# Block 3's transpose moved from TensorE to the DMA, and the first loads in another order

## The chip, the cores and the metric

One core of one Trainium2 chip. The metric is the device time of one execution in microseconds (us). Engines: PE is TensorE, DVE VectorE, ACT ScalarE, POOL GpSimd, SP SyncE; SP and ACT issue DMAs through hardware queues, POOL through a software queue.

## The reference, cut to what matters

```python
def reference(A_x, A_wqkv, A_wo, B_x, B_w_in, B_w_sp, B_b_sp, B_w_out):   # S = 2048, D = 512, bf16
    x = A_x
    xn = layernorm(x)
    q, k, v = split(xn @ A_wqkv)           # 32 heads of 16
    # each position attends to itself and 7 earlier ones, 2 apart
    logits = einsum(q, k[pos - 2 * w]) * 16 ** -0.5      # w = 0..7, masked below 0
    a = (softmax(logits) * v[pos - 2 * w]).sum(w) @ A_wo
    z = gelu(xn @ B_w_in)                  # 1792 columns
    z1, z2 = z[:, :896], layernorm(z[:, 896:])
    g = B_w_sp @ z2 + B_b_sp[:, None]      # 2048 x 2048
    return x + a + (z1 * g) @ B_w_out
```

## The kernel before, in words

The 2048 positions are 16 blocks of 128 rows; four blocks make a wave of 512 columns for the products that want positions in the free dimension. Every step is a task of a planner (`Plan`): an engine, a function that emits instructions, an estimated time, a priority (the smaller goes first), and what it reads and writes. `schedule` is a list scheduler run when the kernel is built. It fixes the order of the tasks on each engine and the PSUM banks they use; the chip then follows that order, each engine waiting for semaphores. A table `land` gives the planner landing times for the first loads, and chains of task names near the end of `build_kernel` fix the order at the start by hand.

The start, around the change:

- PE first runs eight dummy matmuls (`warm0` to `warm7`, six of 512 columns and two of 128; line 566).
- ACT's queue loads blocks 0 and 1 of x (`ldx0`, `ldx1`); SP's loads V's weights in two halves (`ldwv0`, `ldwv1`), block 2, z2's weights in two halves (`ldwin2a`, `ldwin2b`), blocks 3 to 7, Q's and K's weights (`ldq`, `ldk`, 512 KB each) and blocks 8 to 15.
- Each block is normalised on DVE: `bnst`, `bnag`, `vpe` (statistics), a power on POOL (`rstd`, line 618), `norm` (line 630). PE needs the normalised block turned, with the features in the partitions (`xnT`). For blocks 0 to NXT-1 = 3 PE turns it by four matmuls with the identity (`xTr`, line 585), and ACT copies it out of PSUM (`xTe`, line 593). For blocks from 4 on, SP issues a DMA transpose (`xTd`, line 624).
- For blocks 0 to 2, V is made ahead of the normalisation: PE turns the raw block (`xTx`, line 585 too), ACT copies it (`xTc`, line 612), PE multiplies by V's weights (`V0_0` and so on, line 673; a `cs` task at line 645 sums the weights' columns, and ACT copies that out as `cse`), and a DVE step (`fix`, line 682) puts the mean right.
- `z2_b_0`, `z2_b_1` (line 785) multiply block b by the two halves of z2's weights; ACT applies the gelu (`z2g`). `Q0_c`, `K0_c` (line 696) are Q and K of the first wave, four groups c; they need `xnT` of blocks 0 to 3 and Q's and K's weights. `Q1_c` and `K1_c` need blocks 4 to 7.

After that: products of Q and K on DVE and their sums over a head on PE (`red`, line 732), softmax, V gathered by DMA and multiplied on DVE (line 955), z1 (line 831), the big product with w_sp (line 927) and the output (lines 983 and 992). PE goes through them in the planner's order.

`bbc` and `w_sp` are loaded after the transposes in `lnd[NXT:]`, that is of blocks 4 to 15.

Of the kernel before, what the change touches and what calls it, by code (L numbers as in the profile page):

```python
# [36 lines left out]
class Plan:  # L37
# [85 lines left out]
    def schedule(self, dma_bw=300.0, xbar_bw=190.0, dma_lat=1300.0, dma_pre=400.0, issue=None, tol=40.0, land=None,  # L123
# [49 lines left out]
        while left:  # L173
            pick = None
            for e in ENGS:
                sc = []
                for t in cand[e]:
                    r = max(t.ready, free[e])
                    for b in t.banks:
                        if b.base is None:  # L180
                            p = place(b)
                            if p is None:
                                r = None
                                break
                            r = max(r, p[2])
                    if r is not None:
                        sc.append((r, t))
                if not sc:
                    continue
                st = min(r for r, _ in sc)  # L190
                near = [(t.prio, t.idx, r, t) for r, t in sc if r <= st + tol]
                near.sort(key=lambda x: x[:2])
                r, t = near[0][2], near[0][3]
                if e == "act" and t.tbl is not None and tbl is not None and t.tbl != tbl:
                    stay = [x for x in near if x[3].tbl in (None, tbl)]
                    if stay and stay[0][0] < t.prio + t.late:
                        r, t = stay[0][2], stay[0][3]
                if pick is None or r < pick[0]:
                    pick = (r, e, t)
            if pick is None:  # L200
                raise RuntimeError("scheduler stuck")
            r, e, t = pick
            for b in t.banks:
                if b.base is None:
                    _, o, av = place(b)
                    b.base = o[0]
                    prevs = {id(slots[i]["prev"]): slots[i]["prev"] for i in o if slots[i]["prev"] is not None}
                    for pb in prevs.values():
                        for u in pb.users:
                            if u.eng == e == "pe":  # L210
                                t.odeps.add(u)
                            elif u is not t:
                                t.deps.add(u)
                    for i in o:
                        slots[i]["prev"] = b
            t.start = r
            if t.dma is not None:
                iss = issue[e]
                t.eng_end = r + iss
                bw = xbar_bw if t.dma.get("xbar") else dma_bw  # L220
                xs = max(r + iss + dma_pre, dma_free)
                xe = xs + t.dma["nbytes"] / (bw if xs > 7000.0 else min(bw, 265.0))
                dma_free = xe
                t.end = xe + dma_lat
                if t.name in land:
                    t.end = land[t.name]
                    dma_free = land[t.name] - 500.0
            else:
                dur = t.est
                if t.tbl is not None:  # L230
                    if tbl is not None and t.tbl != tbl:
                        dur += 1300.0
                    tbl = t.tbl
                t.end = r + dur
                t.eng_end = t.end - (overlap if e == "dve" else 0.0)
            free[e] = t.eng_end
            for b in t.banks:
                b.left -= 1
                if b.left == 0:
                    av = max(u.end + (220.0 if u.eng == "pe" else 60.0) for u in b.users)  # L240
                    for s in slots:
                        if s["prev"] is b:
                            s["avail"] = av
            cand[e].remove(t)
            order[e].append(t)
            left -= 1
            for o in t.outs:
                o.ready = max(o.ready, t.eng_end if t in o.odeps else t.end + hop(t, o))
                o.nwait -= 1
                if o.nwait == 0:  # L250
                    cand[o.eng].append(o)
# [87 lines left out]
def build_kernel(nc, A_x, A_wqkv, A_wo, B_x, B_w_in, B_w_sp, B_b_sp, B_w_out, out, report=False, emit=True):  # L339
# [8 lines left out]
    KP = 16  # L348
    NVS = 4
    NPB = 3  # L350
    NXT = 4
    NRAW = 3
    NWARM = 8
    x2 = A_x[0]
    o2 = out[0]

# [3 lines left out]
    off = {}  # L360
# [39 lines left out]
    with ExitStack() as es:  # L400
# [54 lines left out]
        R1(("yout", 3, 384), "yout", 128, 512 * 3 + 384)  # L455
        for s_ in range(NVS):
            R1(("Vs", s_), "Vs", 4096, 4096 * s_)
        R1(("wqk", 0), "wqk", 2048)
        R1(("wqk", 1), "wqk", 2048, 2048)
        for s_ in range(2):  # L460
            R1(("wv", s_), "wv", 1024, 1024 * s_)
        for r_ in range(NWS):
# [33 lines left out]

        def dma(eng, fn, nbytes, chan, reads=(), writes=(), name="", xbar=False, prio=0.0, after=()):
            return T(eng, fn, reads=reads, writes=writes, name=name, prio=prio, after=after,
                     dma=dict(chan=chan, nbytes=nbytes, xbar=xbar))

        ident = A("ident", 128)
        E32 = A("E32", 32)
# [35 lines left out]
                B_w_in[:, 1344:1792].rearrange("(c p) n -> p c n", p=128)),  # L538
                512 * 448 * 2, "w_in2b", writes=["w_in2b"], name="ldwin2b")

        def ld_wqk(which, eng):
            dma(eng, lambda e: e.dma_start(
                AC(off["wqk"] + 2048 * which, [[512, 4], [1, 512]]),
                A_wqkv[:, 512 * which: 512 * which + 512].rearrange("(c p) n -> p c n", p=128)),
                512 * 512 * 2, ("wqk", which), writes=[("wqk", which)], name="ld%s" % ("qk"[which]))

        dma("act", lambda e: e.dma_start(A("xin", 512), x2[0:128, :]), 128 * 512 * 2, ("xin", 0),
            writes=[("xin0", 0), ("xin0", 1)], name="ldx0")
# [1 line left out]
        ld_wv(0)  # L550
        ld_wv(1)
        ld_x(2, "sp")
        ld_win2a()
        ld_win2b()
        ld_x(3, "sp")
        ld_x(4, "sp")
        ld_x(5, "sp")
        ld_x(6, "sp")
        ld_x(7, "sp")
        ld_wqk(0, "sp")  # L560
        ld_wqk(1, "sp")

        bw = plan.bank("warm")
        for wi in range(NWARM):
# [14 lines left out]
        def pe_tr(src, keys, name):  # L579
            bk = plan.bank(name)  # L580

            def tr(t):
                last = None
                for dc in range(4):
                    last = t.matmul(P(bk, 128, 128 * dc), src[:, 128 * dc:128 * dc + 128], ident, start=True,  # L585
                                    stop=True)
                return last
            T("pe", tr, reads=keys + ["ident"], writes=[bk], est=(430.0 if name == "xTx0" else 4 * c_mm(128)), name=name)
            return bk

        def to_xnT(b, bk, halves, prio=0, after=()):
# [98 lines left out]
        def qk_pair(j, c):  # L690
            bk = plan.bank("QK%d_%d" % (j, c), 2)
            for which in range(2):
                def mm(t, which=which):
                    last = None
                    for dc in range(4):
                        last = t.matmul(P(bk, 512, 512 * which),  # L696
                                        AC(off["wqk"] + 2048 * which + 512 * dc + c, [[4, 128]]),
                                        AC(off["xnT"] + dc * S + 512 * j, [[1, 512]]), start=(dc == 0),
                                        stop=(dc == 3))
                    return last  # L700
                T("pe", mm, reads=[("wqk", which)] + [("xnT", b) for b in range(4 * j, 4 * j + 4)], writes=[bk],
                  est=4 * c_mm(512), name="%s%d_%d" % ("QK"[which], j, c), prio=10 + 18 * j + c)
            qo = off["QT"] + 2048 * (j % 2) + 512 * c
            ko = off["KT"] + c * (S + KP) + KP + 512 * j
# [183 lines left out]
        for j in range(NJ):  # L888
            for pr in PAIRS:
# [1 line left out]

        dma("sp", lambda e: e.dma_start(A("bbc", S), bass.AP(tensor=B_b_sp.tensor, offset=B_b_sp.offset,
                                                             ap=[[0, 128], [1, S]])),
            128 * S * 2, "bbc", writes=["bbc"], name="ldbbc", prio=7, after=lnd[NXT:])

        def ld_wT(tc):
            r_ = tc % NWS
            for p_ in range(4):
# [1 line left out]
                dma("sp", (lambda t0, p_: lambda e: e.dma_start_transpose(  # L900
                    AC(off["wT%d" % r_] + 128 * p_, [[512, NB], [1, 128]]), B_w_sp[t0: t0 + 128, :]))(t0, p_),
                    128 * S * 2, ("wT", p_), writes=[("wTs", r_, p_)], name="wT%d_%d" % (tc, p_), xbar=True,
                    prio=6 + tc, after=lnd[NXT:])

        dma("sp", lambda e: e.dma_start(A("w_out", FC * 512).rearrange("p (c n) -> p c n", c=FC),
                                        B_w_out.rearrange("(c p) n -> p c n", p=128)),
# [114 lines left out]

        byname = {t.name: t for t in plan.tasks}
        for names in (["warm%d" % wi for wi in range(NWARM)] +
                      ["xTx0", "cs_0", "V0_0", "xTx1", "cs_1", "V0_1", "xTx2", "V1_0", "V1_1", "xTr0", "V2_0", "V2_1", "xTr1",
                       "z2_0_0", "z2_0_0b", "z2_0_1", "xTr2", "z2_1_0", "z2_1_1", "xTr3", "z2_2_0"],
                      ("rstd4", "Vw0"),
                      ("bnst0", "bnag0", "vpe0", "bnst1", "bnag1", "vpe1", "norm0", "bnst2", "norm1", "bnag2", "vpe2", "norm2",
                       "bnst3", "bnag3", "vpe3", "bnst4", "norm3", "bnag4", "vpe4", "mr", "bnst5", "fix0", "fix1", "fix2"),
                      ["bnst%d" % b for b in range(5, NB)],
                      ("xTc0_0", "xTc0_1", "xTc1_0", "xTc1_1", "xTc2_0", "xTe0_0", "xTe0_2", "Ve0", "xTe1_0", "Ve1", "Ve2",  # L1030
                       "xTe2_0", "z2g0", "xTe3_0", "cse", "z2g1", "z2s0"), ("V10_1", "Q3_3")):
            for n0, n1 in zip(names, names[1:]):
                if byname[n0] not in byname[n1].deps:
                    byname[n1].odeps.add(byname[n0])

        plan.schedule(tol=20.0, dma_bw=300.0, dma_lat=1600.0, overlap=20.0,
                      land=dict(ldx0=3690.0, ldx1=4590.0, ldwv0=4220.0, ldwv1=5320.0, ldx2=5680.0, ldwin2a=8090.0,
                                ldwin2b=9300.0, ldx3=9750.0, ldx4=10060.0, ldx5=10440.0, ldx6=10820.0, ldx7=11250.0, ldq=12740.0, ldk=14220.0))
        if report:
            print("arena", AR, "fp", FR)  # L1040
            plan.report()
# [47 lines left out]
```

## Time and profile before

| | |
|---|---|
| time, median of 3 runs | 237.29 us (236.66 to 237.98) |
| the profiled execution | 236.69 us, span 235.1 us |
| PE busy | 232.2 us (99%) |
| DVE busy | 209.3 us (89%) |
| ACT busy | 97.0 us (41%) |
| DMA | 43.86 MB, mean 187 GB/s |

The profile is of one execution; times in it count from the start of its span, and the execution took 1.6 us more than the span. The busy share of PE counts from a matmul's start to its modelled end, so it says that PE always has a matmul in hand, not that it runs at its peak. A wait is named with what released it; idle time of an engine that holds up nobody costs nothing. A DMA that is issued runs later, so what counts for it is its landing.

### The profile page before, as it was taken

Reading aid. Unit: us, or ns where it says so; the run is one execution under the profiler, and the core shown is the slowest. Engines: PE = TensorE matmul, PEld = TensorE weight load, DVE = VectorE, ACT = ScalarE, POOL = GpSimd, SP = SyncE. Lnnn points to the kernel's source line nnn. Section 1 sums busy time; section 2 is a strip of 40 time slices with the busy share of each in tenths; the row PEclk is TensorE's granted clock in tenths of the full one; section 3 lists DMA queues with packets and bytes.
Section 4 is the critical chain, followed back from the end, with each engine's and each line's share of the span. In section 5 each row is a group of like instructions: output and inputs, shape, how many; then the busy total and the mean of one; then the engine's idle time right before and its main releaser. Section 6 shows DMA issues by size and latency. Waiting matters only on the chain.

```text
span 235.1 us, 3006 instructions
## 1 busy us (share of the span) xinstructions
PE 232.2 (99%) x1139; PEld 109.4 (47%) x1139; DVE 209.3 (89%) x271; ACT 97.0 (41%) x146; POOL 36.0 (15%) x56
## 2 busy tenths in 40 slices
PE   8999999999999999999999999999999999999996
PEld 3555555554444444444444444444444444444443
DVE  4698989999999999979999979989999798999632
ACT  4889889898868985410120134011111111000000
POOL 2268544230644300000000000000000000000000
PEclk9999999999999999999999999999999999999999
DMA  6997929998157314150869999999994949825532
GB/s 208 359 261 180 226 67 159 210 193 201 45 177 248 116 42 70 45 178 0 290 200 298 237 262 206 209 302 273 298 274 129 267 135 284 254 90 140 157 107 67
DMA packets 82013, 43.86 MB, mean 187 GB/s; under 512 B 54336, under 2 KB 81360, under 8 KB 82000
## 3 DMA queue, kind: packets, MB, share of 16 engines
q1 hardware_dynamic: 80768, 41.27, 69.9%
q0 software_dynamic: 800, 2.11, 2.8%
q10 hardware_dynamic: 432, 0.30, 0.4%
q8 instruction: 9, 0.15, 0.3%
q14 instruction: 4, 0.03, 0.0%
HBM read 26.35 MB, written 4.21 MB: 130 GB/s over the span
## 4 chain that ended last, share of the span: by engine, by line
PE 97%; DMA 1%; DVE 0%; issue 0%
PE ps L927 41%; PE ps L696 12%; PE ps L785 10%; PE ps L992 10%; PE ps L831 10%; PE ps L673 6%; PE ps L983 6%; DMA arena<-in_A_wqkv_dram 1%; PE ps L732 1%; PE ps L585 1%; PE ps L645 0%; DVE arena L998 0%
## 5 line engine op out<-in xcount | busy, mean ns | idle before, releaser
L927 PE MATMUL ps<-arena 128*128 128x512 bf16 x448 | 97.0, 379 | 0.0
L927 PEld LDWEIGHTS ps<-arena 128*128 128x128 bf16 x448 | 43.7, 98 | 53.1 <-issue 0.4
L935 ACT ACTIVATE arena<-ps 128x1024 bf16<-128x1024 f32 (+1 forms) x16 | 14.7, 916 | 77.0 <-PE ps L927 71.1
L955 DVE TENSOR_TENSOR arena<-arena 128x4096 bf16<-128x4096 bf16 x16 | 36.5, 2282 | 0.0
L717 DVE TENSOR_TENSOR arena<-arena 128x4096 bf16<-128x4096 bf16 x16 | 36.4, 2281 | 0.1
L958 DVE TENSOR_TENSOR arena<-arena 128x2048 bf16<-128x2048 bf16 (+1 forms) x32 | 30.2, 948 | 0.0
L696 PE MATMUL ps<-arena 128*128 128x512 bf16 x128 | 28.9, 379 | 0.0
L722 DVE TENSOR_TENSOR arena<-arena 128x4096 bf16<-128x4096 bf16 x12 | 27.5, 2288 | 0.1
L992 PE MATMUL ps<-arena 128*128 128x512 bf16 (+2 forms) x119 | 27.0, 366 | 0.0
L785 PE MATMUL ps<-arena 128*128 128x448 bf16 x128 | 25.8, 352 | 0.0
L831 PE MATMUL ps<-arena 128*128 128x512 bf16 x112 | 24.5, 379 | 0.0
L696 PEld LDWEIGHTS ps<-arena 128*128 128x128 bf16 x128 | 14.5, 113 | 13.1
L998 DVE TENSOR_TENSOR arena<-ps,arena 128x512 bf16<-128x512 f32 (+2 forms) x17 | 11.2, 657 | 9.0 <-PE ps L992 8.6
L705 ACT ACTIVATE arena<-ps 128x1024 bf16<-128x1024 f32 x16 | 16.3, 1021 | 3.6 <-PE ps L696 3.3
L785 PEld LDWEIGHTS ps<-arena 128*128 128x128 bf16 x128 | 12.4, 98 | 11.5
L992 PEld LDWEIGHTS ps<-arena 128*128 128x128 bf16 x119 | 11.4, 98 | 12.9
L831 PEld LDWEIGHTS ps<-arena 128*128 128x128 bf16 x112 | 11.0, 98 | 13.2 <-ACT arena L837 0.3
L983 PE MATMUL ps<-arena 128*128 128x512 bf16 (+2 forms) x68 | 16.6, 366 | 0.0
L793 ACT ACTIVATE arena<-ps 128x896 bf16<-128x896 f32 x16 | 14.6, 916 | 3.8 <-PE ps L785 3.7
L673 PE MATMUL ps<-arena 128*128 128x512 bf16 x64 | 16.1, 379 | 0.0
L938 DVE TENSOR_TENSOR arena<-arena 128x1024 bf16<-128x1024 bf16 (+1 forms) x16 | 9.9, 621 | 6.8 <-ACT arena L935 6.8
L837 ACT ACTIVATE arena<-ps 128x1024 bf16<-128x1024 f32 (+1 forms) x16 | 13.9, 922 | 4.9 <-PE ps L831 4.8
(62 smaller groups left out, 180.5 us busy)
## 6 DMA issues: line engine op xcount, KB each, us to landing
arena<-vscr SPq DMA_DIRECT2D x16, 1024.0 KB, 6.0
arena<-in_A_x_dram SPq DMA_DIRECT2D x30, 128.0 KB, 4.0
vscr<-arena POOLq DMA_DIRECT2D x16, 128.0 KB, 3.2
out_dram<-arena SPq DMA_DIRECT2D x15, 128.0 KB, 1.8
arena<-in_A_wqkv_dram SPq DMA_DIRECT2D x2, 512.0 KB, 6.4
arena<-in_B_w_in_dram SPq DMA_DIRECT2D x2, 448.0 KB, 5.6
arena<-in_B_w_in_dram SPq DMA_DIRECT2D x1, 896.0 KB, 6.1
arena<-in_B_w_out_dram SPq DMA_DIRECT2D x1, 896.0 KB, 4.9
```

Of the source, the lines that this page charges most:

```text
L673: last = t.matmul(P(bk, 512), A("xcT", 128, 512 * b + 128 * dc) if b < NRAW else xTv(b, dc), A("wv", 512, 512 * dc), start=(dc == 0), stop ...
L696: last = t.matmul(P(bk, 512, 512 * which), AC(off["wqk"] + 2048 * which + 512 * dc + c, [[4, 128]]), AC(off["xnT"] + dc * S + 512 * j, [[1 ...
L705: T("act", lambda a: a.activation(AC(qo, [[ko - qo, 2], [1, 512]]), P(bk, 1024).rearrange("p (t n) -> p t n", t=2), ACTF.Copy, scale=0.5), ...
L717: T("dve", (lambda pbv, qb, kb: lambda v: v.tensor_tensor(pbv, qb, kb, ALU.mult))(pbv, qb, kb), reads=rd, writes=[("pb", s_)], est=c_tt(40 ...
L722: T("dve", (lambda av, bv: lambda v: v.tensor_tensor(av, av, bv, ALU.add))(av, bv), reads=[("pb", 1)], writes=[("pb", acc)], est=c_tt(4096 ...
L785: last = t.matmul(P(bk, 448, 512 * hf), xTv(b, dc), AC(off["w_in2"] + 896 * dc + 448 * hf, [[1, 448]]), start=(dc == 0), stop=(dc == 3))
L831: last = t.matmul(P(bk, 512, 512 * i), AC(off["w_in1"] + 896 * dc + 128 * fc, [[1, 128]]), AC(off["xnT"] + dc * S + 512 * j, [[1, 512]]), ...
L927: last = t.matmul(P(bk, 512, 512 * i), AC(off["z2"] + FH * sh + 128 * fc, [[1, 128]]), AC(off["wT%d" % r_] + sh * 512, [[1, 512]]), start= ...
L955: T("dve", lambda v: v.tensor_tensor(tv, tv, av, ALU.mult), reads=[("attn", b)], writes=[("Vs", sv)], est=c_tt(4096), name="pv%d" % b, pri ...
L958: T("dve", (lambda n: lambda v: v.tensor_tensor(A("Vs", n, 4096 * sv), A("Vs", n, 4096 * sv), A("Vs", n, 4096 * sv + n), ALU.add))(n), wri ...
L983: last = t.matmul(P(bk, cn), AC(off["OT"] + 512 * tb + 128 * cc, [[1, 128]]), AC(off["wo"] + 512 * cc + c0, [[1, cn]]), start=(cc == 0), s ...
L992: last = t.matmul(P(bk, cn), AC(off["z1T"] + fc * S + 128 * tb, [[1, 128]]), AC(off["w_out"] + 512 * fc + c0, [[1, cn]]), start=False, sto ...
```

## The change

- Block 3 is turned by DMA instead of PE (`NXT` from 4 to 3). `lnd[4:]` keeps the order of the later loads behind the transposes of blocks 4 to 15.
- `ldx3` goes ahead of `ldwin2a` and `ldwin2b` on SP.
- Q's and K's weights come in one transfer of 1 MB, `ldqk`, laid out with Q and K side by side for each 128 rows, from ACT's queue, in ACT's order between `xTc2_0` and `xTe0_0`.
- On SP, `xTd3` goes after `ldx5` and ahead of `ldx6` and of all later blocks.
- Seven dummies instead of eight; the one that goes has 128 columns.
- The hand-written orders of PE, DVE and ACT are adapted.
- The planner asks for as many free pairs of banks as a task needs (before, one pair at a time), and its figures for DMA are others: transposes take SP 1270 or 2200 ns to issue and land 900 ns after their data, 270 instead of 300 GB/s for loads, another `land` table, a tolerance of 35 instead of 20 ns.

```diff
@@ Plan.schedule
-                    for b in t.banks:
+                    need = [b for b in t.banks if b.base is None]
+                    if len(need) > 1:
+                        ok = sorted(max(slots[i]["avail"], slots[i + 1]["avail"]) for i in (0, 2, 4, 6)
+                                    if all(slots[k]["prev"] is None or slots[k]["prev"].left == 0 for k in (i, i + 1)))
+                        r = max(r, ok[len(need) - 1]) if len(ok) >= len(need) else None
+                        need = []
+                    for b in need:
...
-                t.eng_end = r + iss
+                t.eng_end = r + (t.dma.get("iss") or iss)
...
-                t.end = xe + dma_lat
+                t.end = xe + (900.0 if t.dma.get("xbar") else dma_lat)
@@ build_kernel
-    NXT = 4
+    NXT = 3
-    NWARM = 8
+    NWARM = 7
...
-        R1(("wqk", 0), "wqk", 2048)
-        R1(("wqk", 1), "wqk", 2048, 2048)
+        R1("wqk", "wqk", 4096)
...
-                     dma=dict(chan=chan, nbytes=nbytes, xbar=xbar))
+                     dma=dict(chan=chan, nbytes=nbytes, xbar=xbar, iss=(1270.0 if nbytes < 400000 else 2200.0) if xbar else None))
...
-        def ld_wqk(which, eng):
-            dma(eng, lambda e: e.dma_start(
-                AC(off["wqk"] + 2048 * which, [[512, 4], [1, 512]]),
-                A_wqkv[:, 512 * which: 512 * which + 512].rearrange("(c p) n -> p c n", p=128)),
-                512 * 512 * 2, ("wqk", which), writes=[("wqk", which)], name="ld%s" % ("qk"[which]))
+        def ld_wqk(eng):
+            dma(eng, lambda e: e.dma_start(A("wqk", 4096).rearrange("p (c n) -> p c n", c=4),
+                                           A_wqkv[:, 0:1024].rearrange("(c p) n -> p c n", p=128)),
+                512 * 1024 * 2, "wqk", writes=["wqk"], name="ldqk")
...
         ld_x(2, "sp")
+        ld_x(3, "sp")
         ld_win2a()
         ld_win2b()
-        ld_x(3, "sp")
         ld_x(4, "sp")
         ld_x(5, "sp")
         ld_x(6, "sp")
         ld_x(7, "sp")
-        ld_wqk(0, "sp")
-        ld_wqk(1, "sp")
+        ld_wqk("act")
...
-            T("pe", tr, reads=keys + ["ident"], writes=[bk], est=(430.0 if name == "xTx0" else 4 * c_mm(128)), name=name)
+            T("pe", tr, reads=keys + ["ident"], writes=[bk], est=4 * c_mm(128), name=name)
...
-                                        AC(off["wqk"] + 2048 * which + 512 * dc + c, [[4, 128]]),
+                                        AC(off["wqk"] + 1024 * dc + 512 * which + c, [[4, 128]]),
...
-                T("pe", mm, reads=[("wqk", which)] + [("xnT", b) for b in range(4 * j, 4 * j + 4)], writes=[bk],
+                T("pe", mm, reads=["wqk"] + [("xnT", b) for b in range(4 * j, 4 * j + 4)], writes=[bk],
...
-            128 * S * 2, "bbc", writes=["bbc"], name="ldbbc", prio=7, after=lnd[NXT:])
+            128 * S * 2, "bbc", writes=["bbc"], name="ldbbc", prio=7, after=lnd[4:])
...
         for names in (["warm%d" % wi for wi in range(NWARM)] +
-                      ["xTx0", "cs_0", "V0_0", "xTx1", "cs_1", "V0_1", "xTx2", "V1_0", "V1_1", "xTr0", "V2_0", "V2_1", "xTr1",
-                       "z2_0_0", "z2_0_0b", "z2_0_1", "xTr2", "z2_1_0", "z2_1_1", "xTr3", "z2_2_0"],
+                      ["xTx0", "cs_0", "V0_0", "xTx1", "cs_1", "V0_1", "xTx2", "V1_0", "V1_1", "xTr0", "V2_0", "xTr1", "V2_1",
+                       "z2_0_0", "z2_0_0b", "z2_0_1", "xTr2", "z2_1_0", "z2_1_1", "z2_2_0", "z2_2_1"],
                       ("rstd4", "Vw0"),
-                      ("bnst0", "bnag0", "vpe0", "bnst1", "bnag1", "vpe1", "norm0", "bnst2", "norm1", "bnag2", "vpe2", "norm2",
-                       "bnst3", "bnag3", "vpe3", "bnst4", "norm3", "bnag4", "vpe4", "mr", "bnst5", "fix0", "fix1", "fix2"),
+                      ("bnst0", "bnag0", "vpe0", "bnst1", "bnag1", "vpe1", "norm0", "bnst2", "norm1", "bnag2", "vpe2", "bnst3", "norm2",
+                       "bnag3", "vpe3", "norm3", "bnst4", "bnag4", "vpe4", "mr", "bnst5", "fix0", "fix1", "fix2"),
                       ["bnst%d" % b for b in range(5, NB)],
-                      ("xTc0_0", "xTc0_1", "xTc1_0", "xTc1_1", "xTc2_0", "xTe0_0", "xTe0_2", "Ve0", "xTe1_0", "Ve1", "Ve2",
-                       "xTe2_0", "z2g0", "xTe3_0", "cse", "z2g1", "z2s0"), ("V10_1", "Q3_3")):
+                      ("xTc0_0", "xTc0_1", "xTc1_0", "xTc1_1", "xTc2_0", "ldqk", "xTe0_0", "xTe0_2", "xTe1_0", "Ve1", "Ve0", "Ve2",
+                       "xTe2_0", "z2g0", "cse", "z2g1", "z2s0"), ("ldx5", "xTd3", "ldx6"),
+                      *[("xTd3", "ldx%d" % b) for b in range(7, NB)], ("V10_1", "Q3_3")):
...
-        plan.schedule(tol=20.0, dma_bw=300.0, dma_lat=1600.0, overlap=20.0,
-                      land=dict(ldx0=3690.0, ldx1=4590.0, ldwv0=4220.0, ldwv1=5320.0, ldx2=5680.0, ldwin2a=8090.0,
-                                ldwin2b=9300.0, ldx3=9750.0, ldx4=10060.0, ldx5=10440.0, ldx6=10820.0, ldx7=11250.0, ldq=12740.0, ldk=14220.0))
+        plan.schedule(tol=35.0, dma_bw=270.0, dma_lat=1600.0, overlap=20.0,
+                      land=dict(ldx0=3600.0, ldwv0=4120.0, ldx1=4550.0, ldwv1=5230.0, ldx2=5600.0, ldwin2a=8250.0, ldx3=5950.0,
+                                ldwin2b=9450.0, csr=52000.0, ldx4=9850.0, ldx5=10400.0, xTd3=12700.0, ldqk=13300.0))
```

More of the change, by code (lines that the diff above doesn't have):

```diff
@@ L902, in ld_wT @@
                     128 * S * 2, ("wT", p_), writes=[("wTs", r_, p_)], name="wT%d_%d" % (tc, p_), xbar=True,
-                    prio=6 + tc, after=lnd[NXT:])
+                    prio=6 + tc, after=lnd[4:])
         dma("sp", lambda e: e.dma_start(A("w_out", FC * 512).rearrange("p (c n) -> p c n", c=FC),
```

## The prediction

> **What bounds the kernel now.** I read the page's busy shares and its chain first, to see which engine sets the end.
>
> ```profile
> PE 232.2 (99%) x1139; PEld 109.4 (47%) x1139; DVE 209.3 (89%) x271; ACT 97.0 (41%) x146; POOL 36.0 (15%) x56
> ...
> PE 97%; DMA 1%; DVE 0%; issue 0%
> ```
>
> TensorE (PE) is 97% of the chain; the other engines only matter where they make it wait. So the question is where PE waits. The chain of waits in order of time answers that for the start, which the change touches:
>
> ```profile
> 0.80 3.22 DMA arena<-in_A_wqkv_dram
> 4.02 0.05 issue
> 4.07 0.60 PE ps L645 x2
> ...
> 8.62 1.51 PE ps L785 x8
> ...
> 11.87 0.22 PE ps L585 x4
> 12.09 1.51 PE ps L785 x8
> 13.61 0.86 PE ps L673 x4
> 14.47 6.91 PE ps L696 x32
> ...
> 233.19 0.02 issue
> ```
>
> Until 4.02 the chain is V's first weight half landing; from 4.07 to 233.19 every piece is PE. The starts of single matmuls in the trace confirm it: after 4.07 none starts over 0.1 us later than the one before it allows. So a gain must be PE work removed or an earlier landing of V's weights, and any new wait on PE is lost whole. Next I read PE's timeline (start, us, what, idle before and its releaser) for the deadlines:
>
> ```profile
> 0.84 2.89 PE L566 MATMUL ps<-const-bfloat16-1.0 128*128 128x512 bf16 x8 [0.84 <-PEq L1074]
> 3.56 0.39 PE L585 MATMUL ps<-arena 128*128 128x128 bf16 x4
> ...
> 13.44 1.03 PE L673 MATMUL ps<-arena 128*128 128x512 bf16 x4
> ```
>
> Then ACT's and DVE's timelines at the places that the change moves, the landings of line 624 (the DMA transposes), and two stages of a table by microsecond (PEclk, DMA share, GB/s):
>
> ```profile
> 7.57 0.66 ACT L593 ACTIVATE arena<-ps 128x256 bf16<-128x256 f32 x2 [0.49 <-PE ps L585]
> ```
>
> ```profile
> 9.17 0.69 DVE L605 BATCH_NORM_STATS2 fpool<-arena 128x6 f32<-128x512 bf16 x1 [0.93 <-DMA arena<-in_A_x_dram]
> ```
>
> ```profile
> DMA to landing us min/median/max: 2.3/4.0/7.5
> ```
>
> ```profile
> 8.00:9.00 1.00, 1.00 1.07 373
> ...
> 11.00:12.00 1.00, 1.00 1.09 345
> ```
>
> ScalarE (ACT) and VectorE (DVE) have holes of 0.49 and 0.93 us; a DMA transpose takes 2.3 to 7.5 us from issue to landing; and the DMA engines are full. The landing times below are the trace's records of the semaphore increments.
>
> **The change part by part.**
>
> *xTr3 leaves PE.* Four 128-column matmuls, 0.22 us (piece "11.87"), leave a chain without slack: -0.22. Their eviction (0.60 us of ACT) goes too, which costs or gains nothing, since no PE piece waits for it.
>
> *One dummy fewer.* It is a 128-column one, 0.107 us apart from the next. The first real matmul starts at 3.56, x0 landed at 3.50, and the piece behind waits for V's weights until 4.02. Between -0.06 (starting on x0) and 0; since 4.02 stays, I take 0. The cover is the 0.28 us in which PE waits for those weights. The clock: dummies start every 427 ns, the first transposing matmuls every 56 ns, so full speed is there at 3.56 and the missing dummy is the last one at half speed. The Trainium skill ("TensorE: Matmul & The Clock Gate", Part 1) says that a free-running window of about 3.4 us of activity releases the clock; by that rule a shorter run-up may miss a window, which is the third rival. The trace has one such release and no missed one.
>
> *x3 ahead of z2's weights.* 131 KB at 373 GB/s puts both halves of z2's weights back by 0.35. The first landed at 7.52 and its first matmul starts at 8.46: covered by 0.94. The second landed at 8.77, hence 9.12; it is needed at 9.03 (weight load) to 9.21 (matmul of z2_0_1). Q and K's 1 MB on the other queue can overlap its tail: up to 0.3 more. The stall is 0 to 0.35; I take 0.10, nearer the lower end, because a transfer issued at 7.1 hardly has data moving before 8.9 (x1, issued at 1.26, needed 2.7 us to its first increment).
>
> *Q and K in one transfer on ACT's queue.* The issue (0.42 to 0.46 us as for x0 and x1) comes behind xTc2_0, which ends at 7.08, into the hole of 0.49 before xTe0_0 at 7.57: 0. If it took 0.9 (the longest issue among x's loads), xTe0_0 would be 0.4 late; z2_0_0 at 8.46 has 0.5 to spare. SP loses two issues. Landing: x0 to x5, V's and z2's weights had all landed at 9.90; 1.05 MB at 345 to 373 GB/s makes that 12.7 to 12.9, and xTd3 adds some 0.6 at most; with x6 and x7 ahead, K landed at 13.66 before. Needed by Q0 at 14.31 - 0.22 = 14.09: 0 cost, 0.4 to 1.4 to spare.
>
> *Block 3 by DMA.* DVE: bnst3 begins when x3 is there (5.84: x2 landed at 5.46, and the loads of x land 0.38 apart) and bnst2 is done, so bnst3 runs at about 7.15, norm2 ends at 8.25 as now (it waits for POOL's power), then bnag3, vpe3 (0.33), POOL 0.56 and norm3 0.41: done at 9.6, inside the hole of 0.93. SP issues xTd3 behind ldx5, whose issue was over at 5.55, so it waits for norm3, with x6 to x15 queued behind it. From 9.6 the row's 2.3 gives 11.9, its median 13.6; the first transpose of before (issued at 12.73, landed at 18.56, mixed with loads) gives 15.4. It needs 512 packets of 256 B at 18 ns, 0.6 us over 16 engines; alternating with the rest of Q and K's 1 MB it ends with that, about 13.2. V3 wants it at 13.44 - 0.22 = 13.22. Stall 0 to 2.2; I take 0.05, by the byte count.
>
> *x6 to x15 behind xTd3.* Ten loads at 0.44 (median) go out at 10.9 to 15.3, ahead of xTd4 to xTd7 by their priority (0 against 1); these go out at 15.3 to 20.4 instead of 12.7 to 19.2. QK of the second wave starts at 24.24 - 0.22 = 24.02 and needs block 7: about 21.5. Cost 0; the cover is z2_3 and z2_4 (3.0 us). By the longest row (7.5) it would land at 26.6, a stall of 2.6. Statistics of blocks 6 to 15 are up to 3 us later; DVE takes other work then, and its last sums wait for PE (9.0 us idle at line 998), so nothing on PE: 0.
>
> *The planner's figures and the bank rule.* Another order of the same PE work; it costs nothing unless a bank or an input is late. PE has no such wait now; below 0 is excluded, since there is none to remove. 0, at most the 1 us size of one late eviction.
>
> Sum: -0.22 + 0.10 + 0.05 = -0.07. The profiled execution took 236.69 (span 235.1 and 1.6 around it), so 236.62; the median of the runs lies 0.60 above the profiled one, which makes 237.2.
>
> **The rivals.**
>
> *xTd3 lands late (slower).* For it: the first transpose of before took 5.8 us, during which loads shared the engines. Against it: part of that was ten loads ahead of it on its own queue; here there are two. It decides from a landing at 14.6 on (1.4 us after V3 wants it). At 15.4 PE stalls 2.2: 239.4 with the other terms. V3 and Q0 both need block 3 and nothing else is ordered before them, so nothing hides it. Chance 0.13.
>
> *Later transposes late (slower).* Ten more issues stand ahead of them on SP; it decides from block 7 landing after 25.4, and gives up to 239.8. Against it: 2.5 us of spare time. Chance 0.06.
>
> *The clock comes later (slower).* If full speed came as much later as the half-speed stretch seen (0.84 to 3.56, 2.7 us), PE would do 4.07 to 6.26 at half speed and lose 1.1: 238.3, about half a per cent. Against it: the dummies' other 2.6 us stay. Chance 0.04. With the skill's 3.4 us for a window the estimate would be 1.5.
>
> *All covers hold.* 0.22 less and nothing else: 237.1, the same answer by size.
>
> *The change saves more (faster).* It needs 1.2 us; PE has only 0.22 us less work and V's weights still come first on SP. Only their earlier landing or another day's clock start could do it. Chance 0.05.
>
> **How the numbers follow.** Within 0.5% (1.19 us, about what a measurement of this kernel can tell from no change): the forecast and the case where all covers hold, together 0.72. Slower: 0.13 + 0.06 + 0.04 = 0.23. Faster 0.05. Low end: 237.1 less the 0.63 by which the fastest of the runs lies under their median, so 236.4. High end: the first rival to two thirds, 237.2 + 1.6 = 238.8. Below lies about 0.05, above about 0.14.
>
> **What would show it.** Right: PE's chain from 4.07 to the end without a gap, 0.22 us shorter; lines 585 with 24 matmuls; V3's first matmul at 13.2 to 13.4; the second QK wave near 24. Wrong: a PE wait put down to the DMA on the transpose's line or on in_A_wqkv_dram, a wait above 0.4 us at z2_0_1, real matmuls 427 ns apart after 4.07, or DVE releasing PE near the logits.

## The result and the profile after

| | before | after |
|---|---|---|
| median | 237.21 us (9 runs) | 239.04 us (9 runs, 238.10 to 241.75) |
| ratio to before, 95% interval | | 1.0075 [1.0053, 1.0098] |
| the profiled execution | 236.69 us, span 235.1 us | 238.59 us, span 237.1 us |

The change is slower by 0.5 to 1.0%; the same kernel measured a second time (below) gave 1.0035 [1.0005, 1.0064]. Ratios leave out disturbed runs, over 1.5% above a kernel's fastest; medians hold all runs (the last section has a cause of the long ones).

The page of after, busy shares and chain:

```profile
PE 233.5 (98%) x1134; PEld 109.4 (46%) x1134; DVE 208.8 (88%) x271; ACT 96.7 (41%) x145; POOL 37.4 (16%) x56
...
PE 93%; DMA 3%; DVE 2%; POOL 0%; issue 0%; DVEq 0%
```

The five matmuls are gone (1139 to 1134), but PE is 93% of the chain instead of 97%, and DMA 3%. The chain in order of time (start, us, what) shows where the other engines come in:

```profile
8.61 0.56 POOL fpool L621
9.17 0.03 issue
9.20 0.41 DVE arena L633
9.61 0.03 DVE fpool L608
9.64 4.99 DMA arena<-arena
14.63 0.05 issue
14.68 1.04 PE ps L676 x4
15.71 6.91 PE ps L699 x32
22.62 3.78 PE ps L788 x20
```

Up to 14.63 the chain is now the one that leads to block 3's transpose: x0's landing, the statistics on DVE, the power (L621), the normalisation (L633), and a DMA of 4.99 us, the transpose xTd3. From 14.68 on it is PE without a gap, as before. PE's own timeline has the wait:

```profile
0.84 2.83 PE L569 MATMUL ps<-const-bfloat16-1.0 128*128 128x512 bf16 x7 [0.84 <-PEq L1078]
3.59 0.61 PE L588 MATMUL ps<-arena 128*128 128x128 bf16 x4
...
11.45 2.43 PE L788 MATMUL ps<-arena 128*128 128x448 bf16 x12
14.68 1.04 PE L676 MATMUL ps<-arena 128*128 128x512 bf16 x4 [0.79 <-DMA arena<-arena]
```

Two things beside the wait of 0.79 us are to be seen. The group before V3 has 12 matmuls of 448 columns and not 16: the planner put V3 ahead of z2's second half of block 2 (`z2_2_1`, four matmuls, 0.76 us); its table had the transpose land at 12.7. And the first transposing matmuls take 0.61 us and not 0.39: the clock's record shows full speed from 6.69 on, and in the execution of before from 3.55.

Where the 2.0 us went is a sum of two terms: V3 starts at 14.68 instead of 13.44 (1.24 later), and 0.76 of PE work that lay ahead of it now lies behind it; together 2.00. The last matmul of the kernel starts 234.96 - 232.96 = 2.00 later. So in this execution nothing after V3 got faster or slower, and the matmuls ahead of V3 set nothing by their own length: the transpose's landing sets the time. The clock has a hand in it all the same, through the moment at which ACT issues the weights (below).

### The profile page after: what moved, and what is told of

Same layout as the page of the kernel before. It is cut to its first block, busy times and chain, and to the rows that moved or that the text cites. A ratio compares the mean times of both kernels' runs of the same rounds, so it can differ in the third digit from the quotient of the medians.

```text
span 237.1 us, 2989 instructions
## 1 busy us (share of the span) xinstructions
PE 233.5 (98%) x1134; PEld 109.4 (46%) x1134; DVE 208.8 (88%) x271; ACT 96.7 (41%) x145; POOL 37.4 (16%) x56
## 4 chain that ended last, share of the span: by engine, by line
PE 93%; DMA 3%; DVE 2%; POOL 0%; issue 0%; DVEq 0%
PE ps L930 41%; PE ps L699 12%; PE ps L834 10%; PE ps L995 10%; PE ps L788 9%; PE ps L986 6%; PE ps L676 5%; DMA arena<-arena 2%; DMA arena<-in_A_x_dram 1%; PE ps L735 1%; DVE fpool L608 1%; DVE arena L633 1%; POOL fpool L621 0%; DVE arena L1001 0%; DVE fpool L619 0%; DVE fpool L610 0%
## 5 line engine op out<-in xcount | busy, mean ns | idle before, releaser
L938 ACT ACTIVATE arena<-ps 128x1024 bf16<-128x1024 f32 (+1 forms) x16 | 14.7, 917 | 77.7 <-PE ps L930 71.8
L788 PEld LDWEIGHTS ps<-arena 128*128 128x128 bf16 x128 | 12.5, 98 | 11.9
L995 PEld LDWEIGHTS ps<-arena 128*128 128x128 bf16 x119 | 11.4, 98 | 12.9
L796 ACT ACTIVATE arena<-ps 128x896 bf16<-128x896 f32 x16 | 14.7, 918 | 3.6 <-PE ps L788 3.6
L817 POOL TENSOR_TENSOR fpool<-fpool 128x4 f32<-128x4 f32 x4 | 14.3, 3582 | 10.6 <-DVE fpool L814 10.6
```

The source lines that it names most:

```text
L788: last = t.matmul(P(bk, 448, 512 * hf), xTv(b, dc), AC(off["w_in2"] + 896 * dc + 448 * hf, [[1, 448]]), start=(dc == 0), stop=(dc == 3))
L995: last = t.matmul(P(bk, cn), AC(off["z1T"] + fc * S + 128 * tb, [[1, 128]]), AC(off["w_out"] + 512 * fc + c0, [[1, cn]]), start=False, sto ...
```

## The experiments

Theory A: PE waits for block 3's transpose at V3. Theory B: the missing dummy delays the clock. Under A, A1 says that the loads x6 to x15 behind the transpose on SP's queue hold it up, and A2 that Q's and K's transfer does. Under A2, L says it is because ACT issues it late, and Q because it is on a second queue.

This table holds the profiled execution of each kernel, in us from the span's start, as far as block 3 goes through a DMA (so without e3 and e4): when Q's and K's transfer was issued and landed, when xTd3 landed (issued at 9.6 to 10.2 in all), and when V3's first recorded matmul started. Landings are the trace's records of the semaphore increments. Of V3's four matmuls, e1, e2, e13, e14 and e15 have a record of three, so V3 can have started 0.2 us before the time given there.

| kernel | queue, issue | weights landed | xTd3 landed | V3 starts | time |
|---|---|---|---|---|---|
| after | ACT 7.75 | 14.05 | 14.63 | 14.68 | 238.59 |
| e5, after again | ACT 6.97 | 14.64 | 15.21 | 15.26 | 239.19 |
| e1, eight dummies | ACT 7.69 | 15.75 | 16.35 | 16.62 | 241.97 |
| e2, z2_2_1 first | ACT 7.21 | 14.33 | 14.93 | 15.20 | 238.12 |
| e6, x6 held | ACT 7.37 | 13.58 | 14.11 | 14.16 | 238.47 |
| e8, both | ACT 6.52 | 11.95 | 12.39 | 13.25 | 237.50 |
| e12, e2 again | ACT 6.80 | 12.27 | 12.80 | 13.53 | 237.02 |
| e13, issued earlier | ACT 5.81 | 12.23 | 12.71 | 13.08 | 236.79 |
| e11, half the bytes | ACT 6.80 | 11.16 | 12.07 | 12.78 | 236.70 |
| e9, on SP ahead | SP 4.85 | 12.59 | 13.09 | 13.13 | 237.07 |
| e10, e9 and z2_2_1 first | SP 4.87 | 12.32 | 12.79 | 13.84 | 236.96 |
| e15, e10 again | SP 5.18 | 12.42 | 12.94 | 13.70 | 236.59 |
| e14, on SP, late | SP 8.29 | 13.69 | 14.21 | 14.48 | 238.21 |
| e7, on SP behind | SP 12.05 | 18.07 | 12.01 | 12.73 | 242.88 |

**e1_dummies8.** `-    NWARM = 7` / `+    NWARM = 8`.

> The change with the eighth dummy put back, nothing else. Theory A (PE waits for block 3's DMA transpose, and whatever PE loses ahead of that wait is hidden in it): 238.7 to 239.3, V3's first matmul still at about 14.7 us, with a longer wait if the clock comes early. Theory B (the missing dummy made the clock come 3.1 us later and that is the loss): 237.6 to 238.0, full speed from about 3.6.

238.35 us median (236.85 to 241.97), ratio 1.0032 [1.0009, 1.0054]; the clock came at 6.56, with eight dummies. The ratio lies under the change's first one, which A had not expected, but it equals that of the unchanged kernel measured again (e5, 1.0035). So it shows no gain from the dummy; e4 settles B.

**e2_z2_first.**

```diff
-                       ... "z2_1_0", "z2_1_1", "z2_2_0", "z2_2_1"],
+                       ... "z2_1_0", "z2_1_1", "z2_2_0", "z2_2_1", "V3_0"],
```

> The change with z2's second half of block 2 (four matmuls of 448 columns, 0.76 us) ordered ahead of V3 again; nothing else. Theory A: V3 still starts when the transpose has landed, at 14.6 to 14.9, but 0.76 of work lies inside the wait, so 238.1 to 238.5. Theory B: no change, 238.9 to 239.2, for the order of PE work doesn't matter when the loss is the clock's.

237.46 us (236.80 to 238.12), 1.0004 [0.9988, 1.0020]; its repetition **e12_z2_first_again** 237.69 us (237.02 to 238.65), 1.0016 [0.9996, 1.0036].

> The change with z2's second half of block 2 ahead of V3, once more. If the wait at V3 is what the change costs and this order puts 0.76 us of work into it, the median is 0.5 to 1.2 us under the change's, 237.3 to 238.0; if its first run was a matter of chance, 238.4 or more.

Work put into the wait is won back, 0.7 to 1.0 us against e1 and e5 by the medians, as A has it; e2's median lies under the range expected, which was counted from the change's first median. PE still waits where the transpose is late (1.1 us in e2's profile by its records), and not at V3 in e12's, where it landed at 12.80.

**e3_block3_pe.** `NXT = 4` again, `xTr3` ahead of `z2_2_0`, `xTe3_0` ahead of `cse`, and no order of xTd3 on SP; all else as in the change.

> The change with block 3 turned by PE as before, and with the rest of it (x3 ahead, Q's and K's weights in one transfer of ACT's queue, seven dummies, the planner's figures). Theory A: 237.0 to 237.6, no PE wait near V3, unless the clock comes late here, which now shows in full (up to 238.5). Theory B: 238.2 to 238.6 with the clock at about 6.7.

237.80 us (236.69 to 238.91), 1.0012 [0.9989, 1.0035]. Without the transpose the loss is gone within the interval. The time isn't wholly free of waits:

```profile
15.81 1.46 PE L699 MATMUL ps<-arena 128*128 128x512 bf16 x6 [0.54 <-ACT arena L796]
```

The profile puts this wait, at Q0, down to ACT's gelu (L796), but that one's semaphore came at 15.83, when Q0's first matmul (15.81) had started. What had just come is Q's and K's weights, at 15.68; Q0's weight load waits for them too. So here the late transfer shows at Q0, which none of the theories had.

**e4_before_dummies7.** The kernel before with `NWARM = 7`.

> The kernel before with seven dummies, nothing else. Theory A, with the clock's release a matter of chance: 237.0 to 237.5 in the median, as the kernel before. Theory B: 238.2 to 238.6, with the first matmuls after the dummies 427 ns apart until about 6.7 us.

237.28 us, 0.9993 [0.9978, 1.0007]. B falls: the dummy is worth nothing. The profile of e4 shows half speed until about 5.9 us (by the spacing of the matmuls), and yet the median is that of the kernel before.

**e5_change_again.** The changed kernel.

> The changed kernel once more, on the chip of the next three. Theory A (the landing of block 3's transpose, which differs from run to run, sets when V3 starts): a median of 238.3 to 239.1 and single runs from 237 to 242; V3's start in the profile equals the transpose's landing within 0.1 us, whatever the clock's release. If instead the eighth dummy had made the first experiment faster, the median is 238.9 to 239.3 and no run is under 238.

238.46 us (236.62 to 241.50), 1.0035 [1.0005, 1.0064]. A spread of 4.9 us in ten runs, where the kernel before has 1.4 in 25. What PE waited for:

```profile
PE ps L676 <- DMA arena<-arena: 1.9, 1, 1.9
```

**e6_hold_x6.** A semaphore wait on SP.

```diff
+        byname["ldx6"].deps.add(byname["xTd3"])
...
+                      ["ldx%d" % b for b in range(6, NB)] + ["xTd4"]
```

> The change with x6 to x15 held on SP until block 3's transpose has landed (a semaphore wait; they are issued some 3 us later, and the transposes of blocks 4 on behind them). Theory A1 (the 1 KB packets of x6 behind it on the same queue stall the transpose): no 256-byte packet over 500 ns, landing at 12.5 to 13.6 instead of 14.6, PE's wait at V3 0 to 0.9, runs within 1.3 us of each other, median 237.2 to 238.2 if the later loads cost nothing. Theory A2 (Q's and K's 2 KB packets from ACT's queue slow it): landing 14 to 15 as in the change, 238.7 or more.

238.95 us, 1.0048 [1.0023, 1.0073]. The transpose landed at 14.11 with no load behind it, and a packet of it still took 1.03 us: A1 falls as the main cause. The held loads cost too: the second QK wave waited 0.4 us. In the profile of **e8_z2_first_hold** (e2's edit and this one) that cost stands alone:

> Both edits: z2's second half of block 2 ahead of V3, and x6 to x15 held until block 3's transpose has landed. Theory A1: landing at 12.5 to 13.6, before or just at PE's need (13.2 to 14.6, by the clock's release), so nothing is lost: 236.9 to 237.4, at most 0.2% under the kernel before. Theory A2: landing at 14 to 15 and 237.4 to 238.2.

238.88 us, 1.0059 [1.0032, 1.0086]. In its profile the clock came early (by the spacing of the matmuls), ACT issued the weights at 6.52, the transpose landed at 12.39 and V3 waited for nothing; the wait is at the second wave (PE's timeline):

```profile
25.41 1.89 PE L699 MATMUL ps<-arena 128*128 128x512 bf16 x8 [1.20 <-DMA arena<-arena]
```

The landing is no later than A1 had it, and yet the median is above both ranges. The profile is the fastest of e8's ten runs, so what the others waited for isn't shown.

**e7_qk_on_sp.** `ld_wqk("sp")`, ordered `("ldx7", "ldqk", "ldx8")`.

> The change with Q's and K's transfer moved from ACT's queue to SP, behind xTd3, x6 and x7. Theory A1: stalls of 1 us and more stay, landing of the transpose 13.5 to 15. Theory A2: no stall, landing at 12 to 12.7. In both the weights land only at about 16.5, so Q0 waits for them and the median is 239.2 to 240.0.

242.87 us (four runs), 1.0233 [1.0204, 1.0263]; Q0 waited 4.35 us for the weights, more than expected, and the clock dropped behind that wait (last section). The point of the run: with x6 behind it and the transfer not yet moving, the transpose landed 2.38 us after its issue (12.01), no packet of it took over 18 ns, and V3 didn't wait. A2 stands.

**e9_qk_sp_ahead.**

```diff
-        ld_wqk("act")
+        ld_wqk("sp")
...
-  ... "xTc2_0", "ldqk", "xTe0_0", ...   ("ldx5", "xTd3", "ldx6")
+  ... "xTc2_0", "xTe0_0", ...           ("ldx5", "ldqk", "xTd3", "ldx6")
```

> The change with Q's and K's transfer on SP's queue between ldx5 and xTd3, instead of ACT's; PE's order unchanged. Theory A2 (the transpose can end only when the transfer that shares the engines has, and on ACT's queue that transfer starts late, by PE's clock, since it is issued behind xTc2_0): the weights land at 12.5 to 13.2, the transpose 0.3 to 0.8 later, no 256-byte packet over 500 ns before x6 comes; V3 starts at 13.0 to 13.9, and the median is 237.6 to 238.3. Theory A1 (x6 behind the transpose on its own queue stalls it): stalls of 1 to 3 us as in the change, 238.4 to 239.0.

237.07 us (236.75 to 237.43), 0.9988 [0.9975, 1.0001]. One transfer moved to another queue, and so issued 2.9 us sooner, takes the whole loss away, and the spread with it; A2 had expected 237.6 at best. The chain of e9:

```profile
9.64 3.45 DMA arena<-arena
13.09 0.05 issue
13.13 1.04 PE ps L676 x4
14.17 6.91 PE ps L699 x32
```

The transpose is issued at 9.64 as in the change and takes 3.45 instead of 4.99.

**e10_qk_sp_ahead_z2_first** adds e2's edit.

> As the one before, and z2's second half of block 2 ahead of V3. Theory A2: PE waits 0.3 at most at V3, so 237.0 to 237.5, the same as the kernel before. Theory A1: 237.5 to 238.3.

237.04 us, 0.9985 [0.9968, 1.0002].

**e11_half_qk.** Only rows 0 to 255 of the 512 are loaded, from ACT's queue, and used twice; the kernel leaves out the other half.

> The change with only the first half of Q's and K's weights loaded (256 of 512 rows, 512 KB) from ACT's queue, and these used twice; the products of Q and K are not the reference's. Theory A2: the transfer lands 1.3 to 1.5 us earlier than in the change (12.5 to 13.3) and the transpose about 0.5 us behind it; 237.6 to 238.3. Theory A1: the transpose still stalls for 1 to 3 us on x6 and lands 14.5 or later, whatever the transfer does; 238.4 to 239.0.

236.70 us, 0.9980 [0.9966, 0.9994]. The transfer landed at 11.16 and the transpose took 2.43 us, as without any transfer. Better than expected, and the strongest sign for A2: the transfer's last packet was over at 10.86 and the transpose's first one moved at 10.92. What matters is how much of the transfer is left when the transpose's data move.

**e13_qk_act_earlier.**

```diff
-  ... "xTc1_1", "xTc2_0", "ldqk", "xTe0_0"
+  ... "xTc1_1", "ldqk", "xTc2_0", "xTe0_0"
```

> The change with Q's and K's transfer still on ACT's queue but issued one step earlier, ahead of xTc2_0 instead of behind it (about 1 us sooner). Theory L (it is the late issue): it lands about 1 us sooner, 12.5 to 13.5, the transpose 0.5 behind, and the median falls to 237.3 to 238.0. Theory Q (it is the other queue, whose share of the engines is uneven): single runs still spread over 2 us and more, the median stays within 0.6 of the change's, 238.2 to 239.0.

236.93 us (236.76 to 237.64), 0.9986 [0.9973, 0.9999]. Still ACT's queue, one place earlier, and the loss is gone, by more than L had expected: the second queue alone doesn't cost it. **e14_qk_sp_late** is the counterpart: e9 with `byname["ldqk"].deps.add(byname["xTc2_0"])`.

> The transfer on SP's queue ahead of xTd3, as in the version that cured the loss, but held until xTc2_0 has ended, so that it is issued when ACT issued it in the change (7.1 to 7.9). Theory L: it lands at 13.5 to 14.3 and the transpose 0.5 later; median 238.0 to 238.8. Theory Q: no packet of the transpose over 500 ns ahead of x6, landing of the transpose 13.0 to 13.8, runs within 1.2 us of each other, median 237.2 to 237.9.

238.94 us (four runs, 238.21 to 239.30), 1.0070 [1.0046, 1.0094]. SP's queue with a late issue has the whole loss back, so a late issue costs it on one queue too. But e14 is no exact counterpart: it issued at 8.29 in its profile, later than ACT in any (7.75 at most).

Q keeps its part, and the packet records show where. On ACT's queue the issue and the landing don't go together smoothly: the whole transfer landed at 11.95 to 12.27 from issues up to 6.80 (e8, e12, e13), and at 13.57 to 15.75, in no order, from issues at 6.97 to 7.75 (after, e1, e2, e5, e6). In these five, 63 to 98 of the transfer's 512 packets were still to go when the transpose's first packet moved, and the longest packet of the transpose took 1.0 to 3.1 us. With 0 to 49 left (e8, e11, e12, e13) none took over 0.25 us. On SP's queue none took over 0.5 us, though 66 to 82 were left in e9, e10 and e15; in e14 36 were left and the longest took 0.25. So the long packets, and with them the longest waits, go with both, a transfer that isn't over and its place on the second queue; no run was built to take these two apart, and why a packet takes that long isn't shown.

How the time goes is in the table by microsecond (PEclk, DMA share, GB/s at the end of a row). After:

```profile
9.00:10.00 1.00, 1.00 (x10) 0.61 (x8) 0.80 (x2) 1.00 (x4) 0.16 (x1) 1.00 0.71 130
10.00:11.00 1.00, 1.00 (x7) 0.50 (x6) 0.93 (x5) 1.00 (x3) 0.30 (x1) 1.00 0.91 319
...
13.00:14.00 1.00, 0.89 (x5) 0.26 (x3) 0.33 (x2) 1.00 (x4) 0.00 (x0) 1.00 0.86 81
```

e13:

```profile
9.00:10.00 1.00, 1.00 (x8) 0.50 (x6) 0.34 (x2) 1.00 (x3) 0.55 (x1) 1.00 1.06 412
10.00:11.00 1.00, 1.00 (x10) 0.64 (x9) 0.93 (x4) 1.00 (x3) 0.00 (x0) 1.00 0.95 365
```

In the change SP's loads run out at about 9 (SP is waiting for norm3, with x6 to x15 behind it), and Q's and K's megabyte has only begun: 130 GB/s in that microsecond. In e13 it was issued 1.9 us sooner, so it already flowed when the others ended: 412 GB/s. The rest of the delay is at the end, the 81 GB/s from 13 to 14: nine tenths of the transfer's packets had gone out at 12.32 in the change (11.10 in e13), but the last one only ended at 13.68 (11.75). In e5 nearly all of it is there: the first packet moved at 8.20 (8.16 in e13), nine tenths were out at 11.70, and the last one ended at 14.26. What ACT did at that time, after and then e13:

```profile
7.74 0.60 ACT L615 ACTIVATE arena<-ps 128x512 bf16<-128x512 f32 x1 [0.62 <-PE ps L588]
7.75 0.39 ACTq L547 DMA_DIRECT2D arena<-in_A_wqkv_dram  x1
```

```profile
5.81 0.39 ACTq L547 DMA_DIRECT2D arena<-in_A_wqkv_dram  x1
```

ACT issues the transfer behind an eviction that waits for PE's xTx2, and PE reaches xTx2 sooner or later by when its clock is released: the issue came at 6.80 where full speed began at 4.68 (e12), and at 7.75 where it began at 6.69 (after).

**e15_best** is e10 with five rounds.

> Block 3 by DMA, Q's and K's transfer on SP ahead of xTd3, z2's second half of block 2 ahead of V3, once more and with more rounds. If PE no longer waits, what remains is the 0.22 us of PE work that the change removes: 236.9 to 237.2, a ratio of 0.9985 to 0.9995 to the kernel before. If the transpose still ends the wait in some runs, 237.3 to 237.8.

236.88 us (236.37 to 237.40, 12 runs), 0.9976 [0.9963, 0.9990]: 0.1 to 0.4% under the kernel before, faster than both kernels. The 0.22 us of xTr3 are 0.09%, just outside that interval; e10, the same kernel, has an interval that holds it. What the rest is, if there is one, wasn't tried. Its chain has no DMA ahead of V3:

```profile
10.62 3.03 PE ps L788 x16
13.64 0.05 issue
13.70 0.81 PE ps L676 x3
```

## Why the prediction was wrong, point by point

- *xTr3 leaves PE, -0.22:* right. Line 588 has 24 matmuls of 128 columns, and but for z2_2_1 PE's work after V3 is unchanged; with the wait cured, the kernel is faster by about that (e9, e10, e13, e15).
- *One dummy fewer, 0:* right by e4 and e1. But its reason took 3.56 as the time of full speed; that was one early case. The profiles have the release anywhere from 3.55 to 6.69 us, with seven dummies and with eight. The third rival, a missed window as the effect of the dummy, didn't come to pass; a late clock did, by chance, and in the changed kernel it is hidden in the wait for the transpose.
- *x3 ahead of z2's weights, 0.10:* 0 in the changed profile: z2's second weights landed at 8.82, and with the late clock z2_0_0 only began at 9.72. The reason given for the lower end doesn't add up: 7.1 and x1's 2.7 us make 9.8, not 8.9.
- *ACT's issue, 0:* the issue itself cost PE nothing (0.39 us in a hole), but it came at 7.75, not 7.08: ACT issued it 0.01 us after the start of xTc2_0, not behind its end, and xTc2_0 hangs on PE's clock.
- *Landing of Q's and K's weights, 12.7 to 12.9:* wrong, 14.05. This is the step that failed first. It divided bytes by the full rate from 9.90 on, as if the transfer filled the engines from the moment that the others ended; it moved 130 GB/s in its first microsecond, and its last packets dragged on beside the transpose until 13.68. K's landing at 13.66 in the kernel before, which the text gave beside it, was passed too. No run shows 12.7 to 12.9 for a transfer that ACT issues this late; issues up to 6.80 landed at 11.95 to 12.27.
- *xTd3's landing, about 13.2, stall 0.05:* wrong in size by 1.43 us: 14.63, inside the bounds given (11.9 to 15.4). In place of the 0.05 of stall V3 started 1.46 after 13.22. The mechanism was right: "alternating with the rest of Q and K's 1 MB it ends with that". In all twelve profiles in which the whole transfer went ahead of or beside it, it landed 0.44 to 0.60 us behind the weights, in the kernel after 0.58.
- *V3's deadline, 13.22:* wrong. The text took the hand-written list for the whole order and kept z2_2_1 ahead of V3. The list only fixes the order among its own names; V3 isn't one of them, its priority number is lower, and so the planner moved it ahead, with a price of 0.76 us of cover (e2, e12). The two together are the whole miss in the profiled execution: V3 starts 1.31 after the 13.37 that the forecast's sum comes to, and 0.76 of work has moved behind it; 2.07, as the last matmul starts 2.00 later instead of 0.07 earlier.
- *x6 to x15 behind xTd3, 0:* right for the change: block 7 landed at 23.07 (21.5 expected) and the second wave wanted it at 26.24. e6 and e8 show the second rival at work once the loads go out 1.4 to 3.1 us later still: waits of 0.4 and 1.2 us at the second wave; e12, without that, has one of 0.2. (The 5.55 that the text has for the end of ldx5's issue is ldx6's; ldx5's was over at 4.82. Nothing hangs on it, since SP waited for norm3.)
- *The planner's figures, 0:* right; from V3 on PE has no gap, and the reds' two pauses of 0.1 us are those of before.

The first rival (xTd3 late) is what happened. It named the place, V3, and the price at 15.4, and got too small a chance, because the byte count looked like a measurement and was none. The high end hangs on it too, with a slip: two thirds of 2.2 are 1.5, not 1.6, so it should have been 238.7.

## What to carry to other kernels

A step that moves from the bound engine to a queue is worth its saving only if its landing, not its issue, has slack; and the landing here was tied to that of the big transfer that shared the DMA engines, so look first at when each such transfer is issued, on which queue, and what the issuing engine waits for. A big load should be in the queue before the earlier ones run out: here 1.9 us in its issue were worth 0.5 to 0.9% of the kernel. An order that is written out by hand binds only the names in it; look up where the scheduler may put the others.

## What the runs showed of the hardware that was not expected

- *The clock's release comes at another time in each execution.* In the profiles that have a record of the clock full speed begins at 3.55 (before), 4.68 to 4.96 (e7, e9, e11, e12, e13, e15), 5.59 to 5.82 (e2, e3, e6), 6.56 (e1) and 6.69 (after). The kernel before has 236.62 to 238.04 in its runs, and its profiled execution, with the earliest release, is one of its fastest; so the 0.60 us between that execution and the median, which the prediction added without a cause, fits the clock; no run separates it. The Trainium skill ("TensorE: Matmul & The Clock Gate", Part 1) has a free-running window of about 3.4 us; the spread of 3.1 us over the profiles agrees.
- *A wait of some 3 us costs twice.* In e1's profile PE waited 2.8 us at V3 by its records (2.6 if the matmul without a record started with the landing); the granted clock fell to half at 16.80 and came back at 20.21, 3.41 us later, in which PE lost some 1.7 us more (an estimate, half of that stretch). e7, with 4.35 us of waiting, has the same 3.41 us (18.34 to 21.75). The runs of after at 240.82 and 241.75 have a mean granted clock of 0.993, as these two have; e5's profile, with a wait of 1.9 us, has 1.000. No run of e9, e10, e13 or e15 was over 237.7. The Trainium skill, in the same part, says that an idle window brings the half rate back, and has 3.4 us for the window; the traces agree in the length, but in e1 at a wait that was shorter than a window.
- *A DMA transpose of 128 x 512 alone takes 2.4 us* from issue to landing (e7: 2.38, e11: 2.43), and 2.6 (e13) to 6.6 (e1) with the transfer of 1 MB ahead of or beside it. It isn't the transpose's own bytes that take the time: alone, its 512 packets passed within 0.7 us.
- *A megabyte that starts on engines that run empty starts slowly*: 130 GB/s (after) and 67 GB/s (e14) in the microsecond from 9 to 10, against 412 where it follows other loads without a gap (e13). The first packets of 2 KB took up to 0.9 us each in the kernel after, and at most 0.1 in e13. Why wasn't tried.
